# Folded output weights, a denominator product in four column groups and a hand-ordered first mixer, in a fused attention and mixer block

## The chip, the cores and the metric

The kernel runs on one core of one Trainium2 chip. The metric is device microseconds (us) of one execution on that core. All runs were taken beside runs of the kernel before on the same chip. On one core a run counts as slow when it is over 1.5% above the fastest of the same kernel; such runs are told and left out of every comparison. The engines are called as the profile calls them: PE is the tensor engine (TensorE), PEld its weight loads, DVE the vector engine (VectorE), ACT the scalar engine (ScalarE), and SP the engine that issues the large DMAs (SPq is its sequencer).

## The reference, cut to what matters

`S` = 2048 rows, `D` = 1024 columns, 32 heads of 32, and `F` = 3584; everything is bf16.

```python
# _A_ref, linear attention (x is layer-normalised)
pq, pk = phi(q), phi(k)                       # phi(t) = where(t > 0, t + 1, exp(t)) + 1e-6
kv  = einsum("bhsd,bhse->bhde", pk, v)        # one 32x32 matrix a head
z   = einsum("bhsd->bhd", pk)
num = einsum("bhqd,bhde->bhqe", pq, kv)
den = einsum("bhqd,bhd->bhq", pq, z)[..., None] + 1e-6
attention = (num / den).reshape(B, S, D) @ wo
# _B_ref, a mixer over the rows
u = gelu(einsum("bsd,sf->bdf", layernorm(h), w1) + b1)
y = einsum("bdf,fs->bds", u, w2) + b2
# together
h  = x + attention(layernorm(x));  h2 = h + transpose(y)
```

## The kernel before

The kernel goes through these stages, with their times in the profile of before: layer normalisation and the K and V products (to about 125 us), the Q products with numerator and denominator (to about 180 us), the output projection with the statistics of the second normalisation (to 235.5 us), the first mixer product with `w1` (from there to about 405 us) and the second with `w2`. The mixer multiplies 2x2 blocks with seven products instead of eight. The seven are called p1 to p7. In *quads*, which treat two mixer tiles at once, products 1 and 5 are themselves done by an inner scheme of seven products on 256 columns (i1 to i7). The sums of weights that these schemes need are made by VectorE: `sa` for the outer scheme, `is` for the inner.

Attention divides the numerator by the denominator before the output projection. For each of the 16 blocks of 128 rows:

```python
def attn_num_den(i):
    for j in range(ND):                                   # ND = 8
        b, sl = divmod(j, JPB)
        nc.tensor.matmul(nd_ps[:, b, sl * NCOL:(sl + 1) * NCOL],      # NCOL = 128 + 4
                         lhsT=pqT[:, j, i * P:(i + 1) * P], rhs=ndrhs[:, j, :], start=True, stop=True)
    # [cut] ScalarE: rd = exp(-ln(den + eps)); VectorE: o_sb = num * rd
    return o_sb

def attn_transpose(i, o_sb):
    nc.sync.dma_start_transpose(out=pqT[:, :, i * P:(i + 1) * P], in_=o_sb[:])

def out_proj(i):
    # [cut] for each half dc: acc = x (the residual), then 8 matmuls with wo, copy to h_bf, bn_stats
    # [cut] bn_aggr, reciprocal root on ScalarE
    nc.sync.dma_start(h_dram[i][:], h_bf[:])
```

The first mixer starts with two single tiles and goes on with quads:

```python
def run_pair(st, pend, nxt, after1=nop, after5=nop, on_p4=nop, before_p7=nop, on_p7=nop):
    st.p1()
    after1()
    if not pend:                      # the first tile: half of p2 is put between parts of p5
        h = st.nk // 2
        st.p5(list(range(st.nk - 1)))
        st.p2(list(range(h)))
        st.p5([st.nk - 1])
    # [cut]
    after5(); nxt.pre(5); st.p6(); nxt.pre(6)
    # [cut] rest of p2, p7, p3
    return [st]

# first mixer
nxt = Mixer1(1)
pend = run_pair(cur, [], nxt)
cur, nxt = nxt, quad1(1)
pend = run_pair(cur, pend, nxt, after1=sums1, after5=sums5)
for u in range(1, NQ1):
    cur = nxt
    pend, nxt = cur.run(pend, lambda: quad1(u + 1) if u + 1 < NQ1 else None, on_p4=next_load1(u + 1))
```

## Time and profile before

| | before |
|---|---|
| median of the runs | 573.47 us (573.22 to 573.52, 3 runs) |
| span of the profiled execution | 571.5 us |
| last group of K/V matmuls | 124.97 us |
| first mixer matmul | 235.50 us |
| p2 of the first full quad | 271.37 us |
| each later quad | 23.57 us |

From the profile's page of before: busy time of each engine with its share and count; PE's busy tenths and the granted TensorE clock, in tenths, in 40 equal slices; and the engines' shares of the chain of waits.

```profile
PE 563.7 (99%) x3124; PEld 293.3 (51%) x3124; DVE 390.2 (68%) x759; ACT 272.0 (48%) x585; POOL 1.8 (0%) x8
...
PE   7999999999999999999999999999999999999997
...
PEclk9999999999999999999999999999999999999999
...
PE 95%; DVE 3%; ACT 1%; issue 1%; DMA 1%; ACTq 0%
```

PE is busy at 90% or more in all slices but the first and the last, and bounds the kernel. So the question for any change here is what it does to PE's sequence. The timeline of PE shows it, with start, duration, engine, line of the kernel, operation, what it writes and reads, and in brackets the idle time before it and what ended that:

```profile
134.55 0.63 PE L1118 MATMUL nd_ps<-ndrhs,pqT 128*128 128x132 bf16 x8
135.02 3.61 PE L1019 MATMUL acc_t<-xnT,wq_sb 128*128 128x512 bf16 x16
138.47 0.63 PE L1118 MATMUL nd_ps<-ndrhs,pqT 128*128 128x132 bf16 x8
...
235.50 1.68 PE L297 MATMUL psA<-hE,wq 128*128 128x512 f16 x7
237.34 0.38 PE L297 MATMUL psA<-hE,wq 128*128 128x512 f16 x1 [0.15 <-DVE hE L1189]
...
239.96 1.02 PE L297 MATMUL psA<-hO,wq 128*128 128x512 f16 x4 [0.74 <-ACT psB L316]
...
271.37 3.62 PE L297 MATMUL psA<-hO,wq 128*128 128x512 f16 x16
...
294.94 3.62 PE L297 MATMUL psA<-hO,wq 128*128 128x512 f16 x16
```

A PE duration runs 0.16 us into the next group: the sixteen matmuls from 135.02 end at 138.63 us, and the next group starts at 138.47. The price of a group is therefore the step from its start to the next start: eight 132-column matmuls cost 135.02 - 134.55 = 0.47 us, sixteen of 512 columns cost 138.47 - 135.02 = 3.45 us, so 0.216 us each. The seam between projection and mixer shows waits of 0.15 and 0.74 us. Quads start 23.57 us apart.

The DMA view of one `w1` tile's load, whose columns are the GB/s in 40 slices of the 10 us from 287.6:

```profile
GB/s 0 0 0 0 0 0 106 143 221 184 254 381 385 393 385 373 385 385 360 352 344 352 356 332 356 356 336 348 352 344 348 197 53 4 0 0 0 0 0 0
...
wq<-in_B_w_dram SPq DMA_DIRECT2D x2, 1024.0 KB, 6.6
```

### The profile page before, as it was taken

The numbers are of one execution on the slowest core, as the hardware profiler recorded it, in microseconds if no ns is written. First come the engines' busy times: TensorE is split into PE (matmuls) and PEld (weight loads), VectorE is DVE, ScalarE is ACT, GpSimd is POOL, SyncE is SP. The second block draws the span as 40 slices with busy tenths as digits, with TensorE's granted clock in tenths as the row PEclk, the third lists the DMA queues.
The fourth block names the chain that finished last, engine by engine and source line by source line (L and its number), as shares of the span: only waits on it lengthen the run. The fifth ranks groups of instructions, "written<-read, shape, count | busy, mean of one in ns | idle before, by whom it ended". The sixth has DMA issues, their size and how long they took to land.

```text
span 571.5 us, 8308 instructions
## 1 busy us (share of the span) xinstructions
PE 563.7 (99%) x3124; PEld 293.3 (51%) x3124; DVE 390.2 (68%) x759; ACT 272.0 (48%) x585; POOL 1.8 (0%) x8
## 2 busy tenths in 40 slices
PE   7999999999999999999999999999999999999997
PEld 3444444455554444346555565555445655645643
DVE  6898887546767879873735627453979749659625
ACT  4747777666667776445445354453220411311211
POOL 1000000000000000000000000000000000000000
PEclk9999999999999999999999999999999999999999
DMA  9933432029536753104041340413892932912111
GB/s 303 357 76 79 89 74 38 19 96 323 118 72 127 177 178 111 55 2 147 1 148 28 120 148 1 148 48 81 205 255 84 244 96 75 278 56 73 38 47 46
DMA packets 97800, 66.61 MB, mean 117 GB/s; under 512 B 32082, under 2 KB 91744, under 8 KB 97760
## 3 DMA queue, kind: packets, MB, share of 16 engines
q1 hardware_dynamic: 97024, 65.42, 41.7%
q10 hardware_dynamic: 672, 0.66, 0.3%
q8 instruction: 24, 0.39, 0.3%
q14 instruction: 16, 0.13, 0.1%
q0 software_dynamic: 64, 0.01, 0.0%
HBM read 50.34 MB, written 8.39 MB: 103 GB/s over the span
## 4 chain that ended last, share of the span: by engine, by line
PE 95%; DVE 3%; ACT 1%; issue 1%; DMA 1%; ACTq 0%
PE psB L297 10%; PE psC L297 10%; PE acc_t L1019 9%; PE acc_t L1167 9%; PE psC L208 7%; PE psA L297 7%; PE psI L230 7%; PE psB L208 6%; PE psI L208 6%; PE psB L750 4%; PE psC L750 4%; PE psA L750 4%; PE psA L208 3%; PE acc_t L674 2%; PE psE L750 2%; PE psE L297 1%
## 5 line engine op out<-in xcount | busy, mean ns | idle before, releaser
L297 PEld LDWEIGHTS <-sa 128*128 128x128 f16 x436 | 42.6, 98 | 46.8 <-issue 0.7
L1019 PE MATMUL acc_t<-xnT,wq_sb 128*128 128x512 bf16 x256 | 58.0, 379 | 0.0
L1167 PE MATMUL acc_t<-wo_sb,pqT 128*128 128x512 bf16 x256 | 56.1, 379 | 0.0
L208 PEld LDWEIGHTS <-wq 128*128 128x128 bf16 (+1 forms) x357 | 34.5, 98 | 31.3
L297 PEld LDWEIGHTS <-wq 128*128 128x128 bf16 (+1 forms) x324 | 31.6, 98 | 33.1 <-issue 1.0
L208 PE MATMUL psC<-gs,wq 128*128 128x512 f16 (+2 forms) x210 | 45.0, 365 | 0.0
L1167 PEld LDWEIGHTS <-pqT 128*128 128x128 bf16 x256 | 24.8, 98 | 29.0
L1019 PEld LDWEIGHTS <-wq_sb 128*128 128x128 bf16 x256 | 24.5, 98 | 27.4
L166 ACT ACTIVATE e_sb<-acc_t 128x512 bf16<-128x512 f32 x40 | 23.9, 597 | 26.5 <-PE acc_t L1019 24.3
L170 DVE TENSOR_SCALAR e_sb<-e_sb 128x512 bf16<-128x512 bf16 x64 | 18.5, 289 | 25.4 <-ACT e_sb L166 24.8
L208 PEld LDWEIGHTS <-sa 128*128 128x128 f16 x231 | 22.6, 98 | 18.6
L750 PEld LDWEIGHTS <-xs 128*128 128x128 f16 x208 | 20.0, 98 | 23.3 <-DVE xs L736 1.3
L208 DVE TENSOR_TENSOR ot<-ot,hr 128x512 bf16<-128x512 bf16 (+2 forms) x27 | 11.2, 415 | 28.1 <-ACT ot L406 27.7
L333 ACT COPY psC<-psB 128x512 f32<-128x512 f32 x22 | 12.5, 570 | 35.1 <-PE psB L297 21.5
L297 PE MATMUL psB<-hT,sa 128*128 128x512 f16 x112 | 28.4, 379 | 0.0
L441 DVE TENSOR_TENSOR e<-psI,es 128x256 f32<-128x256 f32 x12 | 5.1, 425 | 34.0 <-PE psI L230 34.0
L297 PE MATMUL psC<-hT,wq 128*128 128x512 f16 x112 | 28.3, 379 | 0.0
L750 PE MATMUL psA<-wkv,xnT 128*128 128x512 bf16 x104 | 26.7, 379 | 0.0
L1178 DVE BATCH_NORM_STATS2 hst<-acc_t 128x6 f32<-128x512 f32 x32 | 22.1, 692 | 6.7 <-ACT h_bf L1177 6.5
L297 PE MATMUL psA<-hO,wq 128*128 128x512 f16 x112 | 25.6, 379 | 0.7 <-ACT psB L316 0.7
L297 PE MATMUL psB<-hO,sa 128*128 128x512 f16 x112 | 25.5, 379 | 0.0
L297 PE MATMUL psC<-hT,sa 128*128 128x512 f16 x112 | 25.5, 379 | 0.0
(184 smaller groups left out, 1022.9 us busy)
## 6 DMA issues: line engine op xcount, KB each, us to landing
wq<-in_B_w_dram SPq DMA_DIRECT2D x14, 1024.0 KB, 7.7
wq<-in_B_w_dram SPq DMA_DIRECT2D x8, 1792.0 KB, 9.1
xr<-in_A_x_dram SPq DMA_DIRECT2D x16, 256.0 KB, 3.1
h_dram<-h_bf SPq DMA_DIRECT2D x16, 256.0 KB, 2.2
hr<-h_dram SPq DMA_DIRECT2D x32, 128.0 KB, 2.4
out_dram<-ot SPq DMA_DIRECT2D x31, 128.0 KB, 1.8
x_sb<-in_A_x_dram SPq DMA_DIRECT2D x15, 256.0 KB, 3.2
wkv<-in_A_wqkv_dram SPq DMA_DIRECT2D x2, 1024.0 KB, 9.0
```

Source lines behind the costliest of these rows:

```text
L166: pin(nc.scalar.activation(e_sb[:], src, ACT.Exp))
L170: pin(nc.vector.tensor_scalar(e_sb[:], e_sb[:], 1.0, PHI_EPS, ALU.min, ALU.add))
L208: return (lambda *a, **kw: pin(op(*a, **kw))) if Held.on else op
L230: pe.matmul(ps, lhsT=self.lhs[m][:, k, :], rhs=self.mov[m][:, k, :], start=(start and k == 0), stop=(k == self.nk - 1), skip_group_check=True,
L297: pe.matmul(ps[:, cols], lhsT=lhs[:, k, :], rhs=mv(k)[:, cols], start=(start and k == 0), stop=(k == self.nk - 1), skip_group_check=True,)
L333: nc.scalar.copy(self.C[:], self.B[:])
L441: dve.tensor_tensor(self.sts[m].e[:, self.cols(h)], ps, es, ALU.add)
L674: mm = nc.tensor.matmul(pp[:, 0:CW], lhsT=xnT[:, kt, i * P:(i + 1) * P], rhs=wkv[:, kt, c * CW:(c + 1) * CW], start=(kt == 0), stop=(kt == ...
L750: pin(nc.tensor.matmul(ps[:], lhsT=lhs[:, k, :], rhs=rhs[:, k, :], start=(start and k == 0), stop=(k == hk2 - 1), skip_group_check=True,))
L1019: nc.tensor.matmul(qp[:, 0:SW], lhsT=wq_sb[:, kt, j * P:(j + 1) * P], rhs=xnT[:, kt, u * SW:(u + 1) * SW], start=(kt == 0), stop=(kt == ND ...
L1167: nc.tensor.matmul(ap_[:, 0:CW], lhsT=pqT[:, j, i * P:(i + 1) * P], rhs=wo_sb[:, j, dc * CW:(dc + 1) * CW], start=(j == 0 and not SEED_RES ...
L1178: nc.vector.bn_stats(st[:, dc, :], ap_[:, 0:CW])
```

## The change

It means to do less on PE in attention, by leaving the division by the denominator to the queries and by multiplying the head matrices into the output weights once ("folding") instead of applying them to every row. So the 128 numerator matmuls go. The denominators are now products of their own, 32 output rows each; four of them are placed in the four column groups of the array, meant to run at once (e1 measures whether they do). The reciprocals go through DRAM to be spread over the head's 32 rows. The first mixer becomes a first quad whose two tiles begin with p1, p1, p2, p2, with VectorE's and ScalarE's order fixed by hand (calls through `hv`, `hs`, `ht` and `hd` keep the written order). The diff cut to its core:

```diff
-            def attn_num_den(i):                    # [cut] with attn_transpose
+            def fold(j):
+                for c in range(NDC):
+                    cols = slice(c * CW, (c + 1) * CW)
+                    ps = acc_tile()
+                    ht.matmul(ps[:, 0:CW], lhsT=kvT[:, j, :], rhs=wo_sb[:, j, cols], start=True, stop=True)
+                    (hs.copy if c == 0 else hv.tensor_copy)(wf[:, j, cols], ps[:, 0:CW])
+            def den_mm(u):
+                ps = ndp.tile([P, SW], F32, tag="den", name="den_ps")
+                for o in range(2):
+                    for g in range(4):
+                        j = 4 * o + g
+                        ht.matmul(
+                            ps[g * QR:(g + 1) * QR, :],                       # QR = 32
+                            lhsT=zz[:, j, (1 - o) * HB:(1 - o) * HB + QR],
+                            rhs=pqT[:, j, u * SW:(u + 1) * SW],
+                            start=(o == 0), stop=(o == 1), skip_group_check=True,
+                            tile_position=(0, g * QR),
+                        )
+            # [cut] den_inv: Ln and Exp on ScalarE, store; den_spread: 8 broadcasting loads; scale_q
+            for n, (u, j) in enumerate(q_units[8:]):
+                # [cut]
+                if j == 1:
+                    den(u - 1)
+                    den_spread(u - 1)
+                if n in (4, 5, 10, 11):
+                    load_w1(n // 10, n % 2, pin)         # the second w1 tile in the middle of the Q phase
+            for i in range(NS):                          # output projection
+                seed(i + 1); out_mm(i)
+                if i == 0:
+                    load_xr(XRL + 1)
+                    den(NSC - 1)
+                    for k in range(XRL + 2, XRL + XR2 + 1):
+                        load_xr(k)
+                if i == 2:
+                    den_spread(NSC - 1)                  # behind two result stores
+                # [cut]
+                if i == NS - 1:
+                    h_scale(i - 1)
+                    normalize_h(i - 2)
+                    normalize_h(i - 1)
+                out_evac(i)
+                # [cut]
-    pend = run_pair(cur, [], nxt)
-    cur, nxt = nxt, quad1(1)
-    pend = run_pair(cur, pend, nxt, after1=sums1, after5=sums5)
+    Held.on = True
+    sums5()
+    cur.mov5 = mov5
+    pend, nxt = cur.run_first(quad1(1), sums1)
```

The line numbers differ after the change, and most operations that are kept in order carry the line of one helper, L209, so they are told apart by what they write and read.

## The prediction

> **What bounds it.** TensorE. The page has PE busy 563.7 of 571.5 us, and the chain of waits is 95% PE. The time-ordered chain gives the real price of a matmul: 16 of 512 columns take 3.45 us (0.216 each), 4 of 256 columns 0.43 us (0.109), and the Q-phase period of 3.92 us less 3.45 leaves 0.47 us for the eight 132-column numerator/denominator matmuls (0.059 each). Counted with these prices, the stretch from 126 us to 235.5 us (rest of Q, output projection) holds 216 + 256 + 128 matmuls, 109.4 us of work in 109.6: no idle time to win there. VectorE (about 83%) and ScalarE (70%) follow behind. Slack is only at the seam: the first pair and its successor, 235.50 to 259.32, hold 104 matmuls = 22.5 us in 23.8 (the timeline shows waits of 0.15 and 0.74 for VectorE's hE and the ScalarE copy of psA to psB), and the next 12.05 us hold 11.3. The later quads take 23.57 us for 23.35 of work, so their new order can give 1 us at most.
>
> **Counts (the instruction orders of both).**
> - Removed: 128 numerator/denominator matmuls, 7.5 us; 16 512-column matmuls of the first product 5, 3.45 us. Also 48 VectorE evictions (23 us), 16 transposing DMAs.
> - Added: 16 fold matmuls, 3.45 us; 28 256-column matmuls (product 5 of the first two as an inner seven-product), 3.05 us; 8 transposes, about 0.5 us; 32 denominator matmuls of 32x512.
> - Moved: sums of the first weights into the Q phase, normalisation and its reciprocal root by one block, evictions in the first mixer later.
>
> **The disputed term** is the denominators. Serially they cost 32 x 0.216 = 6.9 us and the change would lose. They sit in four column groups. [...] I estimate about 3 us for all 32[...].
>
> PE sum: -7.5 - 3.45 + 3.45 + 3.05 + 0.5 + 3.0 = about -1.0 us. All of it is on the critical path. The seam should return a further 1.5 to 2 us: two Mixer tiles begin with first and second products for both, 6.9 us of work, which covers the last statistics, normalisation, combination and sums on VectorE (about 7 us). ScalarE and VectorE work, more or less of it, costs nothing while five rotating PSUM tiles absorb it; folding steps (2.16 us) ask about 1.8 us of ScalarE, so small stalls around the denominators' two activations (about 1.2 us) are possible. The denominator spread (8 DMAs of 128 KB a time, through HBM) has 6 or more steps before it is needed.
>
> **Predicted: 570.4 us, 8 in 10 between 567.4 and 573.9.** Faster by over 2%: 0.03; within 2%: 0.95; slower: 0.02.
>
> **Right if:** Q phase and projection together shorten by about 1 us; each denominator group takes 0.6 to 1.0 us between neighbouring matmuls; PE idle after the projection's end under 0.3 us; quads after it unchanged near 23.5 us.
> **Wrong if:** denominator groups take 1.7 us (serial); PE waits at a fold for ScalarE, VectorE or the output weights; the first w1 tile, queued behind the first spread, lands after about 156 us, holding VectorE and the accumulators; scaled q arrives late for the projection; the hand-set VectorE order in the first mixer opens a gap per quad.

## More of the kernel before

`next_load1` loads the next `w1` tile, 2 x 1 MB, once a buffer has come free. The sums of that tile are the first VectorE work of the next quad.

The chain of waits, followed in order of time (start, duration, what), says how p2 came to wait:

```profile
238.01 0.62 DVE hst L1178
238.65 0.22 DVE mv_all L1179
238.90 0.30 ACT hln_l L1181
239.22 0.20 ACT sc_all L1182
239.43 0.49 ACT psB L316
```

The last block's statistics, their aggregate, two ScalarE activations and a ScalarE copy stand in a row before p2 may start at 239.96.

## The result, and the profile after

| | before | after |
|---|---|---|
| median | 573.39 us (573.22 to 573.52, 4 runs) | 571.35 us (571.14 to 572.52, 4 runs) |
| ratio | 1 | 0.9969 (0.9951 to 0.9986) |
| span of the profiled execution | 571.5 us | 570.7 us |

A ratio is the mean time of one kernel's fast runs over that of the other's of the same rounds, so it is not quite the ratio of the medians quoted. The profiled execution of after was its slowest, 572.52 us. That matters below.

The page of after:

```profile
PE 562.1 (98%) x3049; PEld 289.9 (51%) x3064; DVE 388.2 (68%) x734; ACT 274.1 (48%) x573; POOL 1.8 (0%) x8
...
PEclk9999999999999999999999999999999999999999
...
PE 87%; DVE 5%; DMA 4%; ACT 2%; issue 1%; SPq 0%; DVEq 0%
PE acc_t L209 16%; PE psC L209 14%; PE psB L209 12%; PE psI L209 11%; PE psA L209 6%; PE psB L797 4%; PE psC L797 4%; PE psA L797 4%; DMA wq<-in_B_w_dram 3%; PE acc_t L721 2%; PE psB L299 2%; PE psA L299 2%; PE acc_t L1066 2%; PE psE L797 2
```

The chain's shares have changed: DMA holds 4% instead of 1%, and the last line shows 3% of it with the load of a weight tile (`wq<-in_B_w_dram`). PE's timeline of after:

```profile
131.18 3.62 PE L209 MATMUL acc_t<-xnT,wq_sb 128*128 128x512 bf16 x16
134.73 0.61 PE L209 MATMUL den_ps<-pqT,zz 128*32 128x512 bf16 x8
135.28 1.90 PE L209 MATMUL acc_t<-xnT,wq_sb 128*128 128x512 bf16 x8
...
234.48 3.87 PE L209 MATMUL psA<-hE,wq 128*128 128x512 f16 x16
238.74 3.61 PE L209 MATMUL psA<-hO,wq 128*128 128x512 f16 x16 [0.39 <-ACT psB L318]
...
268.93 3.62 PE L209 MATMUL psA<-hO,wq 128*128 128x512 f16 x16
...
292.83 3.62 PE L209 MATMUL psA<-hO,wq 128*128 128x512 f16 x16
...
305.84 0.60 PE L209 MATMUL psI<-hi,is 128*128 128x256 f16 x4 [0.97 <-ACT psI L242]
...
317.64 2.54 PE L209 MATMUL psA<-hO,wq 128*128 128x512 f16 x11
```

The denominator group `den_ps` takes 135.28 - 134.73 = 0.55 us for eight matmuls. The step into it is longer, too: it starts 134.73 - 131.18 = 3.55 us after the sixteen matmuls ahead of it, which cost 3.45 elsewhere. So a group costs 0.65 us in all. At the seam, p1 to p2 takes 238.74 - 234.48 = 4.26 us, where sixteen matmuls cost 3.45. The first quads follow at 23.90 and 24.81 us instead of 23.57.

Where the time went, from the starts in the two traces (differences of after minus before, us). The third column is a later run with the same instruction counts and only a load moved (e5 below), whose profiled execution took 571.20 us, as the unprofiled ones of after do:

| stretch | after | e5 |
|---|---|---|
| start to the last K/V matmuls | +0.09 | +0.06 |
| Q phase and output projection | -1.11 | -1.11 |
| seam and first mixer products, to p2 of the first full quad | -1.42 | -1.42 |
| from p2 of the first to p2 of the last of the six full quads, five steps | +1.57 | +0.29 |
| the rest | +0.10 | +0.10 |
| sum | -0.8 | -2.1 |

The medians differ by 2.04, so e5's column is probably close to what the usual execution does. The profiled execution of after lost 1.57 us in the quads.

The seam of after on all engines, in order of time:

```profile
235.31 0.43 DVE L209 TENSOR_TENSOR hT<-hO,hT 128x512 f16<-128x512 f16 x1
235.66 0.54 DVE L209 TENSOR_SCALAR hE<-h_bf,mv_all,sc_all 128x1024 f16<-128x1024 bf16 x1
236.11 1.28 DVE L209 BATCH_NORM_STATS2 hst<-acc_t 128x6 f32<-128x512 f32 x2
...
237.43 0.21 DVE L209 BATCH_NORM_AGGREGATE mv_all<-hst 128x2 f32<-128x12 f32 x1
237.68 0.29 ACT L209 ACTIVATE hln_l<-mv_all,eps 128x1 f32<-128x1 f32 x1 [2.41 <-DVE mv_all L209]
...
238.11 1.06 ACT L318 COPY psB<-psA 128x512 f32<-128x512 f32 x2
```

VectorE makes the combination sums of the pair before (`hT<-hO,hT` and the three operations ahead of it), then the normalisation of block 14 (`hE`), and only then the statistics of block 15 (`hst`, `mv_all`). ScalarE, in its fixed order, waits 2.41 us for these with `hln_l`, and the copy `psB<-psA` that p2 needs stands behind it. `hE` ends at 236.20, too, while p1's eighth matmul, which reads it, was due at 234.48 + 7 x 0.216 = 235.99; this is most of p1's stretch.

The first VectorE sums of each next tile in the quads of after:

```profile
271.71 0.43 DVE L209 TENSOR_TENSOR is<-wq 128x512 f16<-128x512 bf16 x1 [1.58 <-DMA wq<-in_B_w_dram]
...
296.52 0.43 DVE L209 TENSOR_TENSOR is<-wq 128x512 f16<-128x512 bf16 x1 [2.49 <-DMA wq<-in_B_w_dram]
```

They wait for the weight tile's DMA. That load, in the 10 us from 286:

```profile
GB/s 0 0 0 0 160 127 131 262 270 352 352 356 360 360 377 373 365 369 360 356 352 344 356 344 348 356 344 344 340 176 25 20 20 25 20 25 20 25 20 16
...
q8 instruction: 1, 0.02, 1.5%
...
wq<-in_B_w_dram SPq DMA_DIRECT2D x2, 1024.0 KB, 8.8
```

Up to the slice of 176 GB/s this is the load of before. Then it trickles at 16 to 25 GB/s for 2.5 us more. The last column of the view is the median over the two halves of the tile, from the issue of each: 8.8 us, where the load of before had 6.6. The second halves, which complete the tile, landed after 10.0 and 7.9 us. There is one transfer more in the window, from the queue that the profile calls "instruction".

### The profile page after: what moved, and what is told of

Its sections match the earlier page's. It is cut to its first block, busy times and chain, and to the rows that moved or that the text cites. A ratio compares the mean times of both kernels' runs of the same rounds, so it can differ in the third digit from the quotient of the medians.

```text
span 570.7 us, 8133 instructions
## 1 busy us (share of the span) xinstructions
PE 562.1 (98%) x3049; PEld 289.9 (51%) x3064; DVE 388.2 (68%) x734; ACT 274.1 (48%) x573; POOL 1.8 (0%) x8
## 4 chain that ended last, share of the span: by engine, by line
PE 87%; DVE 5%; DMA 4%; ACT 2%; issue 1%; SPq 0%; DVEq 0%
PE acc_t L209 16%; PE psC L209 14%; PE psB L209 12%; PE psI L209 11%; PE psA L209 6%; PE psB L797 4%; PE psC L797 4%; PE psA L797 4%; DMA wq<-in_B_w_dram 3%; PE acc_t L721 2%; PE psB L299 2%; PE psA L299 2%; PE acc_t L1066 2%; PE psE L797 2%; PE psC L299 2%; PE kvps L750 1%
## 5 line engine op out<-in xcount | busy, mean ns | idle before, releaser
L209 PEld LDWEIGHTS <-wq 128*128 128x128 bf16 (+1 forms) x653 | 63.4, 98 | 55.6 <-issue 1.0
L209 PEld LDWEIGHTS <-sa 128*128 128x128 f16 x651 | 63.7, 98 | 54.7
L209 PE MATMUL acc_t<-wo_sb,pqT 128*128 128x512 f16 x256 | 55.6, 379 | 0.0
L209 PEld LDWEIGHTS <-is 128*128 128x128 f16 x376 | 36.7, 98 | 19.4 <-issue 4.6
L209 PE MATMUL psC<-gs,wq 128*128 128x512 f16 (+2 forms) x210 | 45.0, 365 | 0.0
L209 PE MATMUL acc_t<-xnT,wq_sb 128*128 128x512 bf16 x188 | 43.1, 379 | 0.2
L209 PEld LDWEIGHTS <-pqT 128*128 128x128 bf16 x256 | 25.0, 98 | 30.5 <-issue 0.6
L209 DVE TENSOR_TENSOR ot<-ot,hr 128x512 bf16<-128x512 bf16 (+2 forms) x27 | 11.2, 414 | 28.1 <-ACT ot L431 27.7
L209 DVE TENSOR_TENSOR e<-psI,es 128x256 f32<-128x256 f32 x20 | 8.5, 424 | 31.9 <-ACT es L255 19.3
L209 PEld LDWEIGHTS <-wq_sb 128*128 128x128 bf16 x192 | 18.5, 98 | 23.0 <-issue 1.3
L209 PE MATMUL psB<-hT,sa 128*128 128x512 f16 x112 | 28.7, 379 | 0.0
L209 DVE BATCH_NORM_STATS2 hst<-acc_t 128x6 f32<-128x512 f32 x32 | 21.3, 692 | 8.7 <-ACT h_bf L209 8.6
L209 DVE TENSOR_TENSOR psA<-psI,es 128x256 f32<-128x256 f32 x18 | 7.8, 433 | 26.9 <-PE psI L209 21.8
L209 PE MATMUL psA<-hO,wq 128*128 128x512 f16 x112 | 25.3, 379 | 0.4 <-ACT psB L318 0.4
L242 ACT COPY psI<-psI 128x256 f32<-128x256 f32 x19 | 6.9, 361 | 38.8 <-PE psI L209 38.8
L209 PE MATMUL psB<-hO,sa 128*128 128x512 f16 x112 | 25.3, 379 | 0.0
L209 PE MATMUL psC<-hT,sa 128*128 128x512 f16 x112 | 25.3, 379 | 0.0
```

The source lines that it names most:

```text
L209: return (lambda *a, **kw: pin(op(*a, **kw))) if self.always or Held.on else op
L242: nc.scalar.copy(self.b, self.a)
```

## The experiments

Two theories stood after the result. **T1**: the attention side gives its 1 us and the mixer's new order gives the rest, all of it visible in PE's sequence. **T2** (rival): the folding is worth little or nothing, and the gain comes from the mixer's order alone, or from the placing of DMAs. For the lost time in the quads: **Q1**: an instruction fetch (so I call a transfer of the queue "instruction") that falls into a weight load delays it. **Q2** (rival): the new VectorE order, or the spread of the denominators, does it by itself. In all 12 runs, outputs were correct. Differences are from the kernel before of the same rounds: 573.33, 573.15 and 573.13 us in the three sessions.

### e0: after again

No edit.

> The changed kernel once more, as the control of this set, because its four runs spread from 571.14 to 572.52 us and the profiled one was the slowest. If the stall of 0.97 us at 305.8 us in its trace (a late weight tile) belongs to that one execution, the new trace lacks it and the times sit near 571.3; if it belongs to the kernel, the new trace has it as well and 571.3 is a time with it.

Measured: median 571.29 us (571.11 to 574.11, six runs), ratio 0.9971 (0.9953 to 0.9988). The gain of 2.04 us repeats. The profiled execution was again one of the slower, 572.21 us, and lost 1.26 us in the quads (23.98 and 24.42 for the first two).

### e1: the denominators without column groups

```diff
-                            ps[g * QR:(g + 1) * QR, :],
-                            lhsT=zz[:, j, (1 - o) * HB:(1 - o) * HB + QR],
+                            ps[:],
+                            lhsT=zf[:, j, :],          # 128 wide, zero outside its rows
-                            start=(o == 0),
-                            stop=(o == 1),
+                            start=(j == 0),
+                            stop=(j == ND - 1),
-                            tile_position=(0, g * QR),
```

> The denominators with full-width stationaries (128 columns, zeros elsewhere), so the same 32 matmuls run one after another and not in four column groups. Theory (the four groups run at once, and PE work is all on the critical path): each group of eight goes from 0.55 to 1.73 us, 4 x 1.18 = +4.7 us against the changed kernel, so about 576 us, slower than the kernel before. Rival (the Q phase has slack that hides this work): within 1 us of the changed kernel.

Measured: 575.54 us (575.25 to 576.81), ratio 1.0041 (1.0029 to 1.0053), 4.25 us over e0. PE's timeline of this run:

```profile
134.59 1.89 PE L209 MATMUL den_ps<-pqT,zf 128*128 128x512 bf16 x8
136.32 1.89 PE L209 MATMUL acc_t<-xnT,wq_sb 128*128 128x512 bf16 x8
```

A group now takes 136.32 - 134.59 = 1.73 us instead of 0.55, and the longer step into it is gone: in this trace the matmuls ahead of it take the usual 0.216 us each. Against the 0.65 us that a group costs in after, four groups make 4 x 1.08 = 4.3 us (the 4.7 us expected left that step out), and the first mixer matmul and its p2 came 4.25 us later. So this added PE work is all on the critical path, and the four column groups are worth more than the whole gain: without them the change loses.

### e2 and e3: each half of the change alone

e2 keeps the new attention and projection and takes the old mixer start and order; e3 keeps the old attention and projection and takes the new mixer. Both are made of the diff's own parts:

```diff
 e2, against after:
-    pend, nxt = cur.run_first(quad1(1), sums1)
+    pend = run_pair(cur, [], nxt)
+    cur, nxt = nxt, quad1(1)
+    pend = run_pair(cur, pend, nxt, after1=sums1, after5=sums5)
-            for f in (n.i1, after1, 0, n.i6, n.i2, 1, n.i5, n.i7, flush, 2, n.i3, 3, n.i4, flush):
+            for f in (n.i1, 0, n.i6, n.i2, 1, n.i5, n.i7, 2, n.i3, 3, n.i4):
 e3, told against after (its recorded edit is against before):
-            def fold(j):                     # and den_mm, den_spread, scale_q
+            def attn_num_den(i):             # and attn_transpose, out_proj of before
```

> Attention and projection of the change, with the mixer start of the kernel before (first two products one after the other, no hand-set order in the mixer). Theory (the gain is the sum of about 1.1 us from the Q phase and projection and about 1 us from the seam and the first products): about 572.3 us. Rival (the attention part gives all the 2.0 us): 571.4. Rival (the attention part gives nothing, what its PE work saves is lost at the seam): 573.4.

> Attention and projection of the kernel before, with the mixer of the change: first two weights as one quad, hand-set order, late evictions, sums of the first weights in the last ten projection blocks. Theory (parts add): about 572.4 us, the seam's stall of about 0.9 us gone and product 5 as an inner product saving 0.4 us. Rival (the hand-set order costs a gap per quad that offsets it): 573.4 or more, with quads above 23.6 us in the trace.

Measured: e2 574.49 us (574.05 to 575.59), ratio 1.0022 (1.001 to 1.0034); e3 571.28 us (571.06 to 571.56), ratio 0.9962 (0.995 to 0.9974). The mixer's half alone gives -2.05 us, as much as the whole change. The attention half alone is 1.16 us slower than before. They do not add: -2.05 + 1.16 = -0.89, but together they give -2.04.

The traces say why. In e2, p2 of the first full quad starts at 270.19, which is 1.18 us earlier than before: the attention saves its 1 us. It then loses 1.68 us in the quads (24.41, 24.30 and 23.68 us for the second to fourth), and the start of the mixer has a PE gap of 0.75 us that waits for VectorE's `hE`. In e3, the first mixer matmul starts at 235.19, p2 of the first full quad at 269.15, and all quads take 23.57. So a kernel with the fold and one without reach the same time. In the profiles, Q phase and projection take 1.1 us less in after than in e3, but its seam and first products take 0.5 us more (34.45 against 33.96), its quads lose to a late tile, and e3 happened to reach its last K/V matmuls 0.4 us earlier (124.63 against 125.06), in code that the change leaves alone. T2 is right about the sum, but not about the fold: its 1.1 us are there, and are lost elsewhere. Where the seam and the late tile are mended (e10 below), the kernel with the fold gains 3.30 us on its own before, against e3's 2.05.

### e4: the last spread at once

```diff
                     den(NSC - 1)
+                    den_spread(NSC - 1)
                     for k in range(XRL + 2, XRL + XR2 + 1):
                         load_xr(k)
-                if i == 2:
-                    den_spread(NSC - 1)
```

> The spread of the last denominators issued at once in the first projection block, not behind two result stores. Theory (its tiles are needed only in blocks 6 to 8, some 12 us later, and the stores have nothing waiting on them): the same as the changed kernel within 0.3 us, 571.3. Rival (the queue blocks on the reciprocals and delays stores and loads of x that the seeds need): 0.5 us or more slower, with a TensorE gap in the projection.

Measured: 575.36 us (574.16 to 576.13), ratio 1.0036 (1.0023 to 1.0049): 4.3 us slower than after, relative to its own before. It was run on another chip. My expectation was wrong. Its timelines show a gap of 2.70 us on PE in the projection, the ScalarE line in front of it, and then a clock that was granted only in part (the last fence has two lines of tables by windows, each with the window, its length, busy time and count of PE, PEld, DVE, ACT and POOL, then the granted clock, DMA share and GB/s):

```profile
202.32 36.38 PE L209 MATMUL acc_t<-wo_sb,pqT 128*128 128x512 f16 x160 [2.70 <-ACT acc_t L209]
```

```profile
200.28 1.07 ACT L209 CAST h_bf<-acc_t 128x512 bf16<-128x512 f32 x2 [4.67 <-DMA h_dram<-h_bf]
```

```profile
202.00:206.00 4.00, 3.68 (x12) 1.40 (x12) 3.39 (x9) 3.69 (x9) 0.00 (x0) 0.67 0.61 234
...
203.40:206.70 3.30, 3.30 (x9) 1.22 (x8) 3.13 (x8) 2.29 (x6) 0.00 (x0) 0.50 0.29 111
```

The spread, the residual rows and the result stores are issued one after the other by SP's sequencer. With the spread first, a residual load was issued at 189.95 (184.57 in after), and the first result store at 194.55 (189.61). That store then took 5.65 us to land, hardly more than in after (5.49), so what came late is its issue. ScalarE's copy to `h_bf`, which has four buffers, waited 4.67 us for that store. PE stood for 2.70 us. Its clock was then 0.67 over the 4 us from 202 and 0.90 over the next 4; these are means, and inside them lies one stretch of about 3.4 us at 0.50, from 203.35 on, with full clock around it. So 160 matmuls took 36.38 us instead of about 34.7 (160 steps of 0.216 and the 0.16 by which a duration runs over). The two make 4.4 us in the profiled execution, whose mean clock was 0.997. Of the five runs, 574.16 and 575.04 us show a mean clock of 1.000 and the other three 0.997, so the loss of clock is not in every execution. "Behind two result stores" is therefore not a detail: it keeps the spread out of the stores' way.

### e5: the second weight tile earlier

```diff
-                if n in (4, 5, 10, 11):
-                    load_w1(n // 10, n % 2, pin)
+                if n in (4, 5, 6, 7):
+                    load_w1((n - 4) // 2, n % 2, pin)
```

> The second weight tile loaded right behind the first, not in the middle of the Q phase. Theory (neither tile is needed before the first mixer products, the second not before 255 us; only the second spread waits behind it): the same as the changed kernel within 0.3 us, 571.3. Rival (2 MB more in front of the second spread makes the scaled q or the first sums late): a gap in the Q phase, 0.5 us or more slower.

Measured: 571.20 us (571.05 to 571.63), ratio 0.9966 (0.9952 to 0.9979). It was run on another chip. No difference that these runs can show. The tile is not needed for long after either place.

### e6: the last block's statistics before the combination sums

```diff
                 if i == NS - 1:
                     h_scale(i - 1)
-                    normalize_h(i - 2)
+                    normalize_h(i - 2, False)      # without its combination sums
                     normalize_h(i - 1)
                 out_evac(i)
+                if i == NS - 1:
+                    combine_h(i - 2)
```

> The changed kernel with one swap in the last projection block: the sums of block pair 6 are made after the statistics of the last block, not ahead of them. Theory (at the seam TensorE waits because normalisation of block 14 and the copy of the first product sit behind those sums: 0.25 us in the first products and 0.55 us ahead of the second ones): second products start at about 238.0 instead of 238.74 us, time 0.5 to 0.8 us less, about 570.6 us unless the late weight tiles take it back. Rival (those sums are needed at once and the wait moves to the inner product): the start of the inner product stays at 242.2 and the time is the same.

Measured: 570.50 us (569.86 to 570.74), ratio 0.9952 (0.994 to 0.9965): -2.65 us, so 0.6 more than after's -2.04. The intervals overlap, but all five runs lie below the ten of after and e0. Its PE timeline has no wait at the seam:

```profile
234.34 3.62 PE L209 MATMUL psA<-hE,wq 128*128 128x512 f16 x16
237.79 3.62 PE L209 MATMUL psA<-hO,wq 128*128 128x512 f16 x16
```

p1 to p2 takes 237.79 - 234.34 = 3.45 us. The 0.81 us that after spent there are gone. So the wait at the seam was one of order on VectorE and ScalarE, not of work.

### e7, e8, e9: moving the instruction fetches

The queue called "instruction" had 24 transfers of 16 KB, against 6128 TensorE instructions (weight loads and matmuls) in the program of after: one for each 255 or so. So the place of a fetch in time should follow from how many TensorE instructions went before. The traces agree, roughly: in all 14, two such transfers lie 177 to 334 TensorE instructions apart, 254 in the mean. The number of warm-up matmuls at the start was changed to move all later fetches, without touching the rest: 48 of 64 columns instead of 10 of 512 in e7 (on after) and e9 (on e6), to move fetches out of the loads, and 33 of 96 columns in e8 (on e3), to move them in.

```diff
-            warm_up(10)
+            warm_up(48, 64)        # e7 on after, e9 on e6;  warm_up(33, 96) in e8 on e3
```

> The changed kernel with 48 warming matmuls of 64 columns instead of 10 of 512, which puts 76 more TensorE instructions ahead of everything and about the same time. Theory [...]: no tail of about 20 GB/s behind the loads of the second and third quad, VectorE's wait for the tile under 1 us in both, quads of 23.6 us, 1.0 us less, about 570.2 us. Rival (the loads are late for a reason of memory or of what the new attention left in the queues): tail and waits as before, time within 0.3 us of 571.3, plus whatever the start costs.

> The reverse, on the kernel with the old attention and the new mixer, whose loads were all undisturbed: 33 warming matmuls of 96 columns, 46 more TensorE instructions, so the fetches, which fell about 9 us after each load's issue, fall about 4 us earlier, into the loads. Theory: tails of about 20 GB/s, VectorE waits of 1 to 2.5 us for the tiles, one or more TensorE gaps of 0.3 to 1 us in the quads, time 0.5 to 2 us more, about 572.3. Rival (the fetches are innocent): quads stay at 23.57 us and the time within 0.3 us of 571.3.

> Both mends together, the swap at the seam and the 48 short warming matmuls. If both causes are right and independent, 0.6 and 1.0 us add: about 569.7 us, faster than both kernels. If only one is right, about 570.3 to 570.7.

Measured: e7 572.87 us (572.42 to 574.04), ratio 0.9999 (0.9985 to 1.0013); e8 574.50 us (573.66 to 575.14), ratio 1.0022 (1.0009 to 1.0035); e9 572.11 us (570.94 to 572.24), ratio 0.9975 (0.9962 to 0.9987). As times all three missed what was expected, and each is slower than the kernel that it was made from, e8 by 3.4 us where 0.5 to 2 were expected. The reason is at the start of the program. PE's timeline of e7:

```profile
5.96 1.03 PE L964 MATMUL tp<-ident,xn 128*128 128x128 bf16 x8 [2.03 <-DVE xn L700]
7.25 3.59 PE L721 MATMUL acc_t<-wkv,xnT 128*128 128x512 bf16 x8 [0.25 <-ACT xnT L974]
```

The warm-up is shorter (2.74 us; 4.45 in after), a gap of 2.03 us follows (0.48 in after), and the first eight products take 3.59 us, where after took 1.90. I call this a cold start. The trace's clock records begin, with full clock, only at 12.13 us here, and at 6.89 us in after, so the clock granted to these first products is not on record. The cold start cost 1.8 us: the first mixer matmul came at 236.29 instead of 234.48. I had kept the count in mind and not the time.

The quads answer the question nevertheless. In e7 and e9, whose loads have no fetch inside, all quads took 23.57 us. In e8 (against 23.57 in e3) three of five became longer, 23.91, 24.19 and 23.72. But the added instructions moved e8's fetches less than expected: four of them start 7.4 to 7.6 us after the issue of the load, where four of e3's start at 7.5 to 8.0. So e8 alone does not show that a fetch moved in makes a load late; what it shows comes under "All tiles together" and after it.

### e10 and e11: the fetches moved with the warm-up kept as long

```diff
-            warm_up(10)
+            warm_up(6)
+            warm_up(40, 64)        # e11 on after, e10 on e6
```

> The changed kernel with this warming alone. Theory: quads of 23.57 us, VectorE waits for the tiles under 0.6 us, seam stall kept: about 570.2 us against 571.3. Rival (the gain of the quads was taken by something else in the earlier shift): 571.3.

> The swap at the seam with the shifted fetches, this time without a cold start: 6 warming matmuls of 512 columns and then 40 of 64, so 72 more TensorE instructions and warming that lasts until the first transposes. Theory (seam 0.8 us and quads about 1 us are independent, the cold first projection cost the earlier shift 1.8 us): first projection matmuls at 7.0 to 7.4 us and 1.90 us for eight, quads of 23.57 us, about 569.4 us, faster than both kernels and than the seam swap alone (570.5). [...]

Measured: e11 570.82 us (570.71 to 570.89), ratio 0.9957 (0.9945 to 0.997); e10 569.83 us over its fast runs (569.71 to 570.12), ratio 0.9941 (0.9927 to 0.9954). They were run on another chip. The profiled run of e10 was a slow one, 590.58 us at a mean clock of 0.949, so its trace is not compared with the others. e10 gains 3.30 us on before and is the fastest kernel.

In e11 the warm-up takes 4.29 us, the gap after it 0.68 us, and the first eight products 1.90 us, as in after. All five quads took 23.57 us. A tile's load in its 10 us from 285.6, and the first sums of the same tiles as shown for after:

```profile
GB/s 0 0 0 0 106 57 139 217 270 365 381 381 389 381 385 389 373 352 352 340 360 348 340 348 356 344 344 356 348 299 66 0 0 0 0 0 0 0 0 0
...
wq<-in_B_w_dram SPq DMA_DIRECT2D x2, 1024.0 KB, 6.5
```

```profile
270.35 0.42 DVE L209 TENSOR_TENSOR is<-wq 128x512 f16<-128x512 bf16 x1 [0.30 <-DMA wq<-in_B_w_dram]
...
293.84 0.43 DVE L209 TENSOR_TENSOR is<-wq 128x512 f16<-128x512 bf16 x1 [0.22 <-DMA wq<-in_B_w_dram]
```

There is no instruction transfer and no trickle at the end; the load lands after 6.5 us (median of its halves), and the sums wait 0.30 and 0.22 us instead of 1.58 and 2.49.

### All tiles together

For every kernel with the new mixer order except e10 (after, e0, e1, e3 to e9 and e11, 55 tile loads) I read from the trace whether an instruction transfer started between 7.2 us ahead of p2, 0.4 us before the issue, and the first sum, when the load landed (median of its halves), how long after the start of p2 the next tile's first sum started (the *lag*), and how much longer than 23.57 us the quad took (the *loss*):

| | loads | landed after | quads that lost more than 0.03 us |
|---|---|---|---|
| no instruction transfer in the load | 27 | 6.5 to 7.0 us | 0 |
| with one | 28 | 6.5 to 8.8 us | 14 |

(Four more transfers had started up to 0.6 us before the issue and ran into the load. They are counted in the first line; none of these loads was late.)

And the loss follows the lag:

| tile | lag us | loss us |
|---|---|---|
| e11, first | 1.49 | 0.00 |
| after, third | 1.79 | 0.00 |
| e0, third | 2.15 | 0.00 |
| e5, second | 2.49 | 0.04 |
| e8, fifth | 2.60 | 0.15 |
| after, first | 2.78 | 0.33 |
| e8, fourth | 3.07 | 0.62 |
| e0, second | 3.30 | 0.85 |
| after, second | 3.69 | 1.24 |

In each losing quad the loss is the lag less 2.45 us, within 0.01. So the new order leaves 2.45 us of slack for a late tile, and everything over it arrives on PE one for one. In e2, with the old order, the same rule holds with 1.90 (2.74 gives 0.84, 2.63 gives 0.73, 2.01 gives 0.11). The largest lag of before was 1.57 us, so it never lost: two of its five loads had a transfer inside, but they landed after 6.6 and 6.4 us. (Its first load landed only after 7.7 us with no transfer inside, but was issued 7.9 us ahead of p2 and had a lag of 0.37.) With the new order no load without a fetch was late, and half of those with one cost PE time. So Q1 holds, on the weight of e7, e9 and e11, where the fetches were moved out and every loss went, with an addition: a fetch in the window is not enough. Nor does its place alone decide: in e8 fetches 7.41 and 7.52 us after the issue cost nothing, and others at 7.40 and 7.59 us cost 0.34 and 0.62. Q2 falls: e3 has the new VectorE order, e7, e9 and e11 have the order and the spread, and all their quads take 23.57 us.

### What stays open

The packets of e8's third load, whose fetch started at 319.15 and took 1.13 us, show more (GB/s in 40 slices of the microsecond from 319, with the fetch, and of that from 320):

```profile
GB/s 328 287 287 287 287 287 819 246 123 287 41 287 41 164 0 123 0 123 41 41 41 0 41 0 0 0 0 0 0 0 0 0 0 0 0 0 0 0 0 0
...
q8 instruction: 1, 0.02, 7.0%
...
GB/s 0 0 0 0 0 0 0 0 0 0 41 0 0 0 0 41 0 0 0 0 0 0 0 0 0 0 0 0 0 0 0 0 0 0 0 0 0 0 0 0
```

Two packets of 1 KB are left over at 319.6, and they move only at 320.25 and 320.38 us, about when the fetch ends (320.28). In the first load of e8 every packet had gone when its fetch, from 7.41 to 8.49 us, was half done. In the trickle of after the packets of 1 KB follow one another almost without overlap: each takes 0.046 to 0.060 us, and the next starts 0.042 to 0.053 us after it. From 293.6 to 295.9 us they are 22 GB/s at a DMA share of 0.07, against 353 GB/s at 1.05 from 288 to 292 us, so about a sixteenth. The profile counts 16 DMA engines, so by these numbers I estimate that one engine's share of the tile was late. The traces do not name the engine of a packet or of a fetch; that it is the engine which carried the fetch, and why other fetches in a load cost nothing, is not shown. Also, the loss in an unprofiled execution can only be judged by times. e11 gains 0.3 us more than after on their own befores, e10 0.65 more than e6, and the intervals overlap in both pairs. The 1.57 us of the profiled execution are more than is usual; e5's 0.29 us are nearer to it.

## Why the prediction was right or wrong

- **The time lay in the range.** 570.4 us was predicted, with 567.4 to 573.9; 571.35 came. The gain is about 0.95 us smaller than predicted.
- **"PE sum about -1.0 us, all of it on the critical path": right as a sum.** Of its terms, -0.40 us (-3.45 + 3.05) belong to the mixer's first products, so for Q phase and projection they make only -0.55. These shortened by 1.11 us, as the "right if" list asked, but partly because the denominators were cheaper than estimated. e1 shows that PE time added in this phase comes out at the end (4.25 us of 4.3).
- **"About 3 us for all 32": somewhat high.** It was my estimate; no trace of before shows such groups. They take 4 x 0.65 = 2.6 us. In four column groups eight matmuls were 1.73 / 0.65 = 2.7 times as fast as one after another in e1, or 1.73 / 0.55 = 3.1 times without the step into the group. Two rounds at 0.216 us would take 0.43 us, so a group costs 0.65 - 0.43 = 0.22 us more than that, 0.10 in the step into it and 0.12 in itself. What this time goes into, the traces do not show.
- **"The seam should return a further 1.5 to 2 us", with "PE idle after the projection's end under 0.3 us": short.** Seam and first products gave 1.42 us, and 0.40 of this is the saving in products that the prediction had already counted in its PE sum. So the waits returned about 1.0 us. That the sum of this and the line before came out near 2.5 us is in part luck: the one was better than its terms, the other worse. PE waited 0.39 us for ScalarE's copy and p1 itself was stretched; p1 to p2 took 0.81 us more than its 3.45 of work. I had covered VectorE's amount of work with 6.9 us of PE work, but not the order: ScalarE's fixed order put the copy for p2 behind the last block's statistics, and VectorE did combination sums before these. e6 shows it: with another order and the same work the 0.81 us are gone.
- **"Quads after it unchanged near 23.5 us": this is the step that failed.** The first two took 23.90 and 24.81 us in the profiled execution, 1.57 us lost in all (0.29 in e5's). The prediction did not reckon with a late weight tile in the quads. Its list of what would make it wrong named a gap per quad from the hand-set VectorE order. But the hand-set order is not to blame: alone (e3) it gives quads of 23.57 us, and it tolerates a later tile than the old one (2.45 us against 1.90). With the 120 TensorE instructions that the change removed (from 6248 to 6128), instruction fetches came to lie in the weight loads of the first two full quads (6.4 and 1.2 us after issue; none in those of before). e7, e9 and e11 moved them out on the same order, and the loss went. In e8 a loss came where e3 had none, with fetches in the loads of both, so e8 supports this more weakly.
- **The risk "first w1 tile lands late" did not come** (it landed at 153.65 us, against the 156 feared), and the second tile's place in the Q phase is worth nothing measurable (e5). The place of the last spread, which the prediction had only counted as early enough, is worth 4 us against the alternative of issuing it at once (e4).

So the gain of 2.04 us is made of about 1.1 us from the fold with column groups, about 1.4 us from the new mixer start, less a few tenths of a late tile. That the mixer's half alone reaches the same time (e3) is because it has no late tile, a smaller wait at its seam and a start that happened to be 0.4 us shorter: its p2 of the first full quad is only 0.22 us later than after's, and its quads lose nothing.

## What to carry to other kernels

Once PE is busy throughout, a change's sum of PE work can be priced from starts in the trace to a few tenths of a microsecond; what is left to find is who starts whom, and for engines with a fixed order one reads what stands in front of the operation that PE waits for. When a quad or loop suddenly takes longer without a change of its own, look at which load came late and whether an instruction transfer lies in its window; here none of the 27 loads without one cost PE time, and 14 of the 28 with one did. In the traces two such transfers lay 177 to 334 TensorE instructions apart, 254 in the mean, so the number of instructions that came earlier went far to set their place. Keep the warm-up's time, not its count, when it is changed (here 2.74 us of it and a gap of 2.03 us were followed by eight products in 3.59 us, and 4.29 us with a gap of 0.68 us by eight in 1.90), and keep small spreading transfers behind the stores whose buffers are needed next (4.3 us in e4).
